# One-bank PSUM tiles in attention and the first MLP, two- and three-bank tiles only in the second, and a longer transfer time in the instruction planner

## The chip, the cores and the metric

One core of a Trainium2 chip runs the kernel as one launch. The metric is the device time in microseconds (us) of that core. A core has five engines with instruction streams of their own: TensorE (PE in the profile, with its weight loads as PEld), VectorE (DVE), ScalarE (ACT), GpSimd (POOL) and SyncE (SP), which here issues the DMA transfers. They wait for each other by semaphores. TensorE writes its products into PSUM, which has eight banks of 128 partitions by 512 fp32 values.

## The reference

All data are fp32. Three stages follow one another: an attention with a block-causal mask, an MLP with a leaky ReLU, and an MLP with SiLU.

```python
# q, k, v: 4 x 8 heads x 576 x 64
scores = (1.0 / np.sqrt(64)) * np.matmul(q, k.transpose(0, 1, 3, 2))
mask = (pos[:, None] // 64) >= (pos[None, :] // 64)
scores = np.where(mask, scores, -1000000000.0)
attn = np.exp(scores - np.max(scores, axis=-1, keepdims=True))
attn = attn / (np.sum(attn, axis=-1, keepdims=True) + 1e-09)
x = np.matmul(attn, v)            # heads joined: 2304 tokens x 512

h = x @ w_in                      # 512 -> 2048
y = np.maximum(0.01 * h, h) @ w_out   # 2048 -> 512

h = y @ w_in2                     # 512 -> 2048
out = (h * (1.0 / (1.0 + np.exp(-h)))) @ w_out2   # 2048 -> 512
```

## The kernel before, in words

**Precision.** Most fp32 products are made from two parts of each factor (a rounded high part and the rest), as three matmuls summed in PSUM; the rounding is done by copies on ACT, DVE and POOL (line L343) and the rests by subtractions (L359). The weights of the second MLP come in as 64-bit words, of which DVE, ACT and POOL make the two parts (the conversions: wraw is the raw load, cy and cc are steps of them; L387 to L416).

**Attention and first MLP.** The 2304 tokens are cut into six blocks of 384. For each block the attention units make scores (L942, L937; in the first block L1123) in a PSUM bank, DVE finds the row maximum (L951; first block L1131, L1142) and masks, ACT takes the exponential out of that bank (L959; first block L1136), and the result meets v (L1000 to L1002). The first MLP then goes through 16 chunks of 128 of its hidden width, with its output in four banks (L1242). Attention of one block is interleaved with the MLP of another.

**Second MLP.** It is multiplied by the Strassen-Winograd scheme: of a pair of chunks and a pair of blocks, seven products instead of eight, in the order 1, 2, 6, 7, 5, 4, 3. The first layer (`add_first`) has 3 x 8 = 24 such pairs, each of 7 products of 6 matmuls of 384 columns (L1471 to L1473); the last (`add_last`, L1634) has five groups of eight pairs, the results summed in PSUM over a group. Product 1 lies in the bank x, products 2 and 6 in s, and products 7, 4, 5 and 3 in acc. After each pair (after each group in the last layer) ACT copies product 1 and DVE combines the products in four steps, each two banks at a time but for the last: `op1` (L1496; products 2 and 6), `op2` (L1499; products 7 and 5), `op3` (L1503; products 4 and 5) and `op4` (L1507; product 3). In the last layer these are L1654, L1660, L1664 and L1669. ACT then applies the SiLU (L1523), and the result goes out to DRAM and comes back for the last layer, as do the converted weights (w2k, L594) and the operands y.

**PSUM.** acc is one tile of four banks for the whole kernel, s one tile of two banks; x and h have one bank each. In attention the scores use the two banks of s by turns, and the first block's transposes use the four of acc by turns.

**What sets the order.** Each engine's stream is ordered by a planner at build time (`class Schedule`): each piece of work has a rank, a cost in ns and the pieces it depends on, and of the pieces that are ready the one with the lowest rank goes next. A transfer counts as its size over 360 bytes per ns and 1500 ns on top (`HOP`). The planner only orders. The semaphores that the chip waits on are made afterwards, from which tiles each instruction reads and writes.

Of the kernel before, what the change touches and what calls it, by code (L numbers as in the profile page):

```python
# [19 lines left out]
P = 128  # L20
# [26 lines left out]
ORDER = (1, 2, 6, 7, 5, 4, 3)  # L47
BEHIND = 6
KQR, KR, QR, VR = 960, 1728, 2048, 1792
# [7 lines left out]
class Task:  # L57
    def __init__(self, engines, deps, rank, emit):
        self.engines, self.deps, self.rank, self.emit = engines, deps, rank, emit
        self.users, self.next, self.waits, self.ready, self.end = [], [], 0, 0.0, None  # L60


class Schedule:
# [23 lines left out]
    def run(self):  # L87
# [20 lines left out]
        while left:  # L108
# [107 lines left out]
def attn_mlp_mlp(  # L216
# [43 lines left out]
    turn_s = [1]  # L260

    def acc_bank(i):
        return acc_all[:, i * 512 : (i + 1) * 512]

# [31 lines left out]
    def next_s():  # L296
        turn_s[0] ^= 1
        return s_all[:, turn_s[0] * 512 : (turn_s[0] + 1) * 512]

# [75 lines left out]

    def convert(src, f, sl, rk, load_rank, to=None, slow=0):

# [39 lines left out]

        t_load = dma(raw_free, load_rank, DM * P * 8, load, after=raw_after, slow=slow)
        raws.takers.append(t_load.issue)
# [169 lines left out]
    def last_raw(f, rk):  # L589

        d, t_x, users = convert(w2, f, slice(DM, 2 * DM), rk, rk - CONV_LOAD / 4)

        def store():
            nc.sync.dma_start(out=w2_kept[f], in_=d["x"])  # L594

        w2_there[f] = dma([t_x], SHORT + rk, P * DM * 4, store)
        users.append(w2_there[f])
# [3 lines left out]
    def last_pair(p, rk, free):  # L601
# [3 lines left out]
        for i in (0, 1):  # L605
# [4 lines left out]
            busy = load_users[p % 2] if p > 1 else y_there[NBLK - 1]  # L610
            t_in.append(dma([w2_there[2 * p + i], *busy], rk - LAST_AHEAD, P * DM * 4, load))
            users.append([])
# [424 lines left out]
    def start():  # L1037
# [318 lines left out]
    def bank(m, n):  # L1356
        if m == 1:
            return x_all[:, :n]
        if m in (2, 6):
            at = (m == 6) * 512  # L1360
            return s_all[:, at : at + n]
        at = (7, 4, 5, 3).index(m) * 512
        return acc_all[:, at : at + n]

    def banks_of(m, n):

        if m == 2:
            return s_all.rearrange("p (k q) -> p k q", q=512)[:, :, :n]
        both = acc_all.rearrange("p (k q) -> p k q", q=512)
        return both[:, 0:3:2, :n] if m == 7 else both[:, 1:3, :n]  # L1370

# [19 lines left out]
    def x_operands(b):  # L1391
# [11 lines left out]
        for k in range(4):  # L1403
# [6 lines left out]
            follow = [t_in[-1].issue] if t_in else []  # L1410
            t_in.append(dma([*y_there[blk][c : c + 2], *free], rk - X2_AHEAD, P * TWO * 4, load, after=follow))

# [44 lines left out]
    def add_first(b, i):  # L1457
# [52 lines left out]
        t1 = plan.add({"DVE": dve_psum(2 * n)}, [t0, t[6], *e_free], r, op1)  # L1510
        t2 = plan.add({"DVE": dve_psum(2 * n)}, [t1, t[5]], r, op2)
        t3 = plan.add({"DVE": dve_psum(2 * n)}, [t2, t[4]], r, op3)
        t4 = plan.add({"DVE": dve_psum(n)}, [t2, t[3]], r, op4)
        bank_free.update({1: [t0], 2: [t1], 6: [t1], 7: [t2], 5: [t3], 4: [t3], 3: [t4]})
        there = []
        first = lambda: d["e0"][:, :n]
        for out_, m, deps, to in (
# [10 lines left out]
            tg = plan.add({"ACT": act(m)}, deps, r, gated)  # L1528
            there.append(dma([tg], SHORT + rk, P * m * 4, store))
        e3_free[k] = [t2, *there]  # L1530
# [12 lines left out]
    def operands4(g, i):  # L1543
# [10 lines left out]
        for side in (0, 1):  # L1554
# [10 lines left out]
            follow = [t_in[0].issue] if t_in else after  # L1565
            t_in.append(dma([*g2_there[i, b], *free], GATE + rk - 3, P * 2 * n * 4, load, after=follow))
        raws.takers.append(t_in[-1].issue)
# [49 lines left out]
    def add_last(g, i):  # L1617
# [54 lines left out]
        t1 = plan.add({"DVE": dve_psum(2 * w)}, [t0, t[6]], r, op1)  # L1672
        t2 = plan.add({"DVE": dve_psum(2 * w)}, [t1, t[5], *c_free["b"]], r, op2)
        t3 = plan.add({"DVE": dve_psum(2 * w)}, [t2, t[4], *c_free["c"]], r, op3)
        t4 = plan.add({"DVE": dve_psum(w)}, [t2, t[3]], r, op4)
        bank_free.update({1: [t0], 2: [t1], 6: [t1], 7: [t2], 5: [t3], 4: [t3], 3: [t4]})
        r0 = 2 * g * TOK
        stored = {}
        for which, at, side, col, dep in (("a", 0, 0, 0, t1), ("c", 0, 1, 0, t3), ("c", 1, 1, 1, t3), ("b", 2, 0, 1, t4)):
# [4 lines left out]

            stored.setdefault(which, []).append(dma([dep], SHORT + rk, P * w * 4, store))
        c_free["a"], c_free["b"], c_free["c"] = [t2, *stored["a"]], [t3, t4, *stored["b"]], stored["c"]
# [126 lines left out]
```

## Time and profile before

| | |
|---|---|
| median of three runs | 1037.62 us (1036.26 to 1041.85) |
| profiled execution | 1036.65 us, its span 1034.9 us, so 1.75 us around it |
| busy in the span | PE 93%, DVE 76%, ACT 54%, POOL 26% |
| attention of the first block | 0 to about 60 us |
| attention and first MLP | about 60 to 620 us |
| second MLP, first layer | about 620 to 839 us |
| second MLP, last layer | about 839 us to the end |

A stage's table of windows says how long each engine was busy in it and at which clock TensorE ran (PEclk, 1.00 is the higher of its two levels). The list of waits sums, for each pair of a waiting line and a line that ended the wait, the idle time. The timeline gives single instructions with, in brackets, the idle time of their engine before them and what ended it. Matmuls overlap, so the distance of two starts, not the duration of one, is what a matmul takes of PE's time.

### The profile page before, as it was taken

The numbers are of one execution on the slowest core, as the hardware profiler recorded it, in microseconds if no ns is written. First come the engines' busy times: TensorE is split into PE (matmuls) and PEld (weight loads), VectorE is DVE, ScalarE is ACT, GpSimd is POOL, SyncE is SP. The second block draws the span as 40 slices with busy tenths as digits, with TensorE's granted clock in tenths as the row PEclk, the third lists the DMA queues.
The fourth block names the chain that finished last, engine by engine and source line by source line (L and its number), as shares of the span: only waits on it lengthen the run. The fifth ranks groups of instructions, "written<-read, shape, count | busy, mean of one in ns | idle before, by whom it ended". The sixth has DMA issues, their size and how long they took to land. (4 is left out here: it accounts for less than half of the span.)

```text
span 1034.9 us, 18465 instructions
## 1 busy us (share of the span) xinstructions
PE 962.2 (93%) x6507; PEld 872.1 (84%) x6507; DVE 785.1 (76%) x1702; ACT 555.0 (54%) x1235; POOL 264.9 (26%) x325
## 2 busy tenths in 40 slices
PE   6788999999999999999999997898889899999997
PEld 3555556899898999899999997888888889999997
DVE  4798898877788878777746696776756788888864
ACT  4678667766777666666645454554345452121222
POOL 1254347212111114011210354323334540000000
PEclk9899999999999999999999998998999999999999
DMA  7576963555665565558424234577635544343422
GB/s 241 170 208 172 212 152 77 129 127 113 141 127 115 135 143 120 117 126 193 114 45 141 72 108 146 184 268 263 207 125 172 176 140 126 125 133 106 139 62 82
DMA packets 193917, 148.81 MB, mean 144 GB/s; under 512 B 134432, under 2 KB 171808, under 8 KB 193824
## 3 DMA queue, kind: packets, MB, share of 16 engines
q1 hardware_dynamic: 193824, 147.63, 52.5%
q8 instruction: 51, 0.84, 0.3%
q14 instruction: 42, 0.34, 0.1%
HBM read 90.44 MB, written 32.51 MB: 119 GB/s over the span
## 5 line engine op out<-in xcount | busy, mean ns | idle before, releaser
L959 ACT ACTIVATE p<-s,st 128x288 f32<-128x288 f32 (+5 forms) x144 | 73.5, 512 | 52.6 <-DVE st L951 33.5
L978 DVE SCALAR_TENSOR_TENSOR hl<-p,st,hl 128x576 f16<-128x576 f32 (+6 forms) x120 | 80.5, 674 | 15.2 <-ACT hl L973 13.4
L1242 PE MATMUL acc<-ghi,w 128*128 128x384 f32 x340 | 88.8, 337 | 0.0
L973 ACT ACTIVATE hl<-p,st 128x576 f16<-128x576 f32 (+6 forms) x118 | 70.0, 598 | 28.5 <-DVE st L969 10.9
L1523 ACT ACTIVATE e<-e 128x384 f32<-128x384 f32 (+1 forms) x72 | 42.9, 627 | 72.1 <-DVE e L1503 52.1
L1270 ACT ACTIVATE g<-h 128x384 f32<-128x384 f32 x96 | 46.6, 486 | 60.0 <-PE h L1224 56.5
L1000 PE MATMUL x<-pt,v 128*128 128x128 f16 (+1 forms) x432 | 69.3, 211 | 6.6 <-DMA pt<-hl 3.5
L359 DVE TENSOR_TENSOR glo<-g,ghi 128x384 fp32r<-128x384 f32 x80 | 53.3, 667 | 26.6 <-ACT ghi L343 25.7
L1001 PE MATMUL x<-pt,v 128*128 128x128 f16 (+1 forms) x432 | 67.1, 209 | 0.0
L1002 PE MATMUL x<-pt,v 128*128 128x128 f16 (+1 forms) x432 | 65.8, 209 | 0.0
L942 PE MATMUL s<-k,q 128*128 128x288 f32 (+7 forms) x256 | 58.7, 331 | 6.2 <-ACT p L959 5.2
L1222 PE MATMUL h<-h,w 128*128 128x384 f32 x180 | 61.1, 339 | 0.0
L1242 PEld LDWEIGHTS acc<-ghi,w 128*128 128x128 f32 x340 | 60.8, 188 | 0.3
L1000 PEld LDWEIGHTS <-v 128*128 128x128 bf16 x432 | 41.3, 98 | 17.9 <-issue 13.0
L1471 PE MATMUL acc<-l,w 128*128 128x384 f32 x90 | 33.5, 372 | 23.0 <-DVE g L1499 22.0
L1242 PE MATMUL acc<-glo,w 128*128 128x384 f32 x160 | 53.7, 336 | 0.3 <-DVE glo L359 0.3
L1224 PE MATMUL h<-h,w 128*128 128x384 f32 x160 | 53.6, 335 | 0.0
L1223 PE MATMUL h<-l,w 128*128 128x384 f32 x160 | 53.6, 335 | 0.0
L359 POOL TENSOR_TENSOR v<-v 128x320 f32<-128x320 f32 (+5 forms) x56 | 39.6, 714 | 51.4 <-DMA v<-vL 44.1
L394 ACT ACTIVATE cy<-wraw 128x512 f32<-128x512 f32 x64 | 42.5, 667 | 18.0 <-DMA wraw<-w 9.2
L1001 PEld LDWEIGHTS <-v 128*128 128x128 bf16 x432 | 41.6, 99 | 9.7 <-issue 9.0
L951 DVE TENSOR_REDUCE st<-s 128x1 f32<-128x320 f32 (+5 forms) x96 | 46.6, 485 | 3.1
(342 smaller groups left out, 3153.7 us busy)
## 6 DMA issues: line engine op xcount, KB each, us to landing
wraw<-w SPq DMA_DIRECT2D x64, 512.0 KB, 4.4
a<-g SPq DMA_DIRECT2D x64, 256.0 KB, 3.2
g<-e SPq DMA_DIRECT2D x48, 192.0 KB, 2.7
g<-e SPq DMA_DIRECT2D x24, 384.0 KB, 2.4
kqr<-kq_l SPq DMA_DIRECT2D x16, 480.0 KB, 3.7
v<-vL SPq DMA_DIRECT2D x32, 160.0 KB, 3.7
y<-yT SPq DMA_DIRECT2D x12, 384.0 KB, 3.6
w2k<-cc SPq DMA_DIRECT2D x16, 256.0 KB, 4.1
```

Of the source, the lines that this page charges most:

```text
L359: engine[e].tensor_tensor(lo, x, hi, op=ALU.subtract)
L942: nc.tensor.matmul(s[:, :w], hd.q[:, a : a + P], hd.k[:, k0:k1], start=i + j == 0, stop=i == len(parts) - 1 and j == 1,)
L959: nc.scalar.activation(p[:rows, k0:k1], u.s[i][:rows, :w], AF.Exp, bias=nm[:rows], accum_out=s2[:rows, i : i + 1])
L973: nc.scalar.activation(hl[:rows, 0, :n], p[:rows], AF.Copy, scale=rc[:rows])
L978: nc.vector.scalar_tensor_tensor(hl[:rows, 1, :n], p[:rows], rc[:rows], hl[:rows, 0, :n], op0=ALU.mult, op1=ALU.subtract)
L1000: nc.tensor.matmul(g.x[:, o], a, hi, start=j == 0, stop=False)
L1001: nc.tensor.matmul(g.x[:, o], hd.vb[:, j], hi, start=False, stop=False)
L1002: nc.tensor.matmul(g.x[:, o], a, lo, start=False, stop=j == nj - 1)
L1222: nc.tensor.matmul(h, w1_lo[s.f][:, sl], hi[:, c, : s.n], start=c == 0, stop=False)
L1223: nc.tensor.matmul(h, w1_hi[s.f][:, sl], lo[:, c, : s.n], start=False, stop=False)
L1224: nc.tensor.matmul(h, w1_hi[s.f][:, sl], hi[:, c, : s.n], start=False, stop=c == NC - 1)
L1242: nc.tensor.matmul(s.acc[c][:, : s.n], a, b, start=s.f == 0 and i == 0, stop=s.f == NF - 1 and i == 2)
```

## The change

No arithmetic is added or taken away. The four-bank acc and the two-bank s no longer exist from the start. In attention each score unit takes a tile of one bank from a pool of two (`ps_s`), and the first block's transposes take one-bank tiles from a pool of four (`ps_t`). When the first MLP starts, the latter gives way to a tile of three banks, acc (products 7, 4 and 5 in the second MLP), and one of a single bank, u (product 3, and the fourth bank of the first MLP's output). When the second MLP starts, the score pool gives way to a two-bank tile s for products 2 and 6. The planner is told that op2 also depends on product 4, and that the bank of product 7 comes free with op3 instead of op2. And it adds 2500 ns (`LAG`) after each transfer of the second MLP: loads of weights and operands, stores and reloads of w2k and of the gated results, and stores of the output.

```diff
-BEHIND = 6
+BEHIND, LAG = 6, 2500
...
-                    u.ready = max(u.ready, t.end + (self.HOP[e] if u in t.users else 0))
+                    u.ready = max(u.ready, t.end + (self.HOP[e] + t.lag if u in t.users else 0))
...
-    acc_all = ps_acc.tile([P, 4 * 512], F32, tag="acc", name="acc")
-    s_all = ps_s.tile([P, 2 * 512], F32, tag="s", name="s")
+    early_s, early_acc = ExitStack(), ExitStack()
+    ps_s = early_s.enter_context(tc.tile_pool(name="ps_s", bufs=2, space=PSUM, side="right"))
+    ps_t = early_acc.enter_context(tc.tile_pool(name="ps_t", bufs=4, space=PSUM))
...
+    banks = {}
+
+    def bank_tile(name, n, side):
+
+        if name not in banks:
+            (early_acc if side == "left" else early_s).close()
+            pool = ctx.enter_context(tc.tile_pool(name=f"ps_{name}", bufs=1, space=PSUM, side=side))
+            banks[name] = pool.tile([P, n * 512], F32, tag=name, name=name)
+        return banks[name]
 
     def acc_bank(i):
-        return acc_all[:, i * 512 : (i + 1) * 512]
+        if i == 3:
+            return bank_tile("u", 1, "left")
+        return bank_tile("acc", 3, "left")[:, i * 512 : (i + 1) * 512]
...
     def next_s():
-        turn_s[0] ^= 1
-        return s_all[:, turn_s[0] * 512 : (turn_s[0] + 1) * 512]
+        return ps_s.tile([P, 512], F32, tag="s", name="s")
...
-    def dma(deps, rank, size, emit, issue=600, after=(), slow=0):
+    def dma(deps, rank, size, emit, issue=600, after=(), slow=0, lag=0):
         t = plan.add({"SP": issue}, deps, rank, lambda e: emit(), after)
         done = plan.add({"DMA": size / 360}, [t], rank, lambda e: None)
+        done.lag = lag
...
-                    u.t = acc_bank(i % 4)
+                    u.t = ps_t.tile([P, 512], F32, tag="t", name="pt0")
...
-            return s_all[:, at : at + n]
-        at = (7, 4, 5, 3).index(m) * 512
-        return acc_all[:, at : at + n]
+            return bank_tile("s", 2, "right")[:, at : at + n]
+        return acc_bank((7, 4, 5, 3).index(m))[:, :n]
...
-        t2 = plan.add({"DVE": dve_psum(2 * n)}, [t1, t[5]], r, op2)
+        t2 = plan.add({"DVE": dve_psum(2 * n)}, [t1, t[5], t[4]], r, op2)
...
-        bank_free.update({1: [t0], 2: [t1], 6: [t1], 7: [t2], 5: [t3], 4: [t3], 3: [t4]})
+        bank_free.update({1: [t0], 2: [t1], 6: [t1], 7: [t3], 5: [t3], 4: [t3], 3: [t4]})
```

The last two edits stand in `add_first` and, alike, in `add_last`; `lag=LAG` stands in the calls of `dma` and `convert` that are named above. Apart from names the streams of all engines are the same up to the first conversions for the second MLP, some 500 us into the run. The lines of the kernel after are 9 or 10 higher than those of the kernel before.

At the start of the second MLP, ACT copies the output of the first MLP's last block out of acc (l is the target) before products 7, 4, 5 and 3 can use these banks; e is a gated result of product 2's and 6's sums, w and cy are weights. Before, ACT's stream reads:

```order
L343 ACTIVATE s1_6913<-x_94 128x384
L343 ACTIVATE w21_1559<-cc_249 128x512
L394 ACTIVATE cy_6940<-wraw_6900 128x512
L1523 ACT_TABLE_LOAD
L1523 ACTIVATE e_6937<-e_6937 128x384
L343 ACTIVATE l_6945<-acc_92 128x384 x4
L394 ACTIVATE cy_6961<-wraw_6909 128x512
```

And now:

```order
L353 ACTIVATE s1_7089<-x_92 128x384
L353 ACTIVATE w22_1637<-t_7066 128x512
L353 ACTIVATE l_7122<-acc_659 128x384
L1532 ACT_TABLE_LOAD
L1532 ACTIVATE e_7119<-e_7119 128x384
L353 ACTIVATE l_7122<-acc_659 128x384 x2
L353 ACTIVATE l_7122<-u_663 128x384
L404 ACTIVATE cy_7157<-wraw_7098 128x512
```

One of the four copies has moved ahead of the load of the activation table and the first SiLU, the three others stay behind both, the last of them from the tile u; the conversion of raw weights that stood before the table load now follows.

On DVE, in the stage of the 24 pairs some 90 us after its start, the conversions of raw weights (cc, cy, wraw) stand between the four combining steps of the pairs (e from s; g from acc; e from acc; e2). Before:

```order
L1507 TENSOR_TENSOR e2_7593<-acc_92,g_175 128x384
L404 TENSOR_SCALAR cc_249<-wraw_7562 128x512
L1496 TENSOR_TENSOR e_6937<-s_93,s1_7591 128x768
L407 TENSOR_SCALAR cc_249<-wraw_7562 128x512
L411 TENSOR_SCALAR cy_7605<-cy_7605 128x512
L404 TENSOR_SCALAR cc_249<-wraw_7571 128x512
L1499 TENSOR_TENSOR g_175<-acc_92,e_6937 128x768
L407 TENSOR_SCALAR cc_249<-wraw_7571 128x512
L1503 TENSOR_TENSOR e_6937<-acc_92,g_175 128x768
L1507 TENSOR_TENSOR e2_7655<-acc_92,g_175 128x384
```

And now, at about the same time of the stage by the pairs:

```order
L369 TENSOR_TENSOR t2_6771<-y_6597,t1_6731 128x768
L421 TENSOR_SCALAR cy_7782<-cy_7782 128x512
L414 TENSOR_SCALAR cc_253<-wraw_7673 128x512
L417 TENSOR_SCALAR cc_253<-wraw_7673 128x512
L1505 TENSOR_TENSOR e_7119<-s_7082,s1_7771 128x768
L1508 TENSOR_TENSOR g_173<-acc_659,e_7119 128x768
L417 TENSOR_SCALAR cc_253<-wraw_7706 128x512
L1512 TENSOR_TENSOR e_7119<-acc_659,g_173 128x768
L1516 TENSOR_TENSOR e2_7850<-u_663,g_173 128x384
```

Before, a step of a conversion (L404) that writes into the area cc stands straight ahead of op2 (L1499), and L407 between op2 and op3. Now nothing stands between op1 (L1505) and op2 (L1508), and one step of a conversion between op2 and op3 (L1512).

On SP's queue at the same place the raw loads (L387), the loads of the operands y for the second pair of blocks (L1407), the stores of converted weights (w2k, L594) and of gated results (g2, L1526) follow each other. Before:

```order
L1526 DMA g2_6_0_129<-e_6937 128x768
L1526 DMA g2_6_0_129<-e2_7440 128x384
L594 DMA w2k6_141<-cc_249 128x512
L1407 DMA y_6418<-yT4_63 128x768
L1526 DMA g2_7_0_132<-e_6937 128x384
L1407 DMA y_6418<-yT5_64 128x768
L1407 DMA y_6418<-yT4_63 128x768
L1526 DMA g2_7_0_132<-e_6937 128x768
L1526 DMA g2_7_0_132<-e2_7531 128x384
L1526 DMA g2_0_1_112<-e_6937 128x384
L387 DMA wraw_7562<-w2 128x512
L387 DMA wraw_7571<-w2 128x512
```

And now:

```order
L1535 DMA g2_7_0_130<-e_7119 128x384
L397 DMA wraw_7673<-w2 128x512
L1416 DMA y_6597<-yT5_64 128x768
L1416 DMA y_6597<-yT4_63 128x768
L397 DMA wraw_7706<-w2 128x512
L1416 DMA y_6597<-yT5_64 128x768
L1535 DMA g2_7_0_130<-e_7119 128x768
L1535 DMA g2_7_0_130<-e2_7709 128x384
L604 DMA w2k5_138<-cc_253 128x512
L604 DMA w2k6_139<-cc_253 128x512
L1535 DMA g2_0_1_110<-e_7119 128x384
L397 DMA wraw_7761<-w2 128x512
```

The loads of raw weights and of y have moved ahead of the stores of the last pair of the first third (g2_7_0), and the stores w2k come later: w2k5 and w2k6 now stand behind the loads of y, where w2k6 stood before them.

## Rows read from the trace of the kernel before

**Rows 1.** Stages: window, length, busy time by engine, PEclk, DMA share, GB/s.

```profile
0.00:60.00 60.00, 43.95 (x213) 28.00 (x214) 37.12 (x114) 35.48 (x98) 13.60 (x23) 0.91 0.63 209
60.00:170.00 110.00, 104.03 (x565) 62.77 (x564) 95.35 (x251) 81.96 (x198) 54.99 (x65) 0.98 0.69 166
620.20:839.20 219.00, 191.68 (x1035) 183.73 (x1034) 155.81 (x223) 104.17 (x180) 85.79 (x65) 0.96 0.56 188
```

**Rows 2.** PE's waits, whole span: waiter, releaser, total us, times, longest.

```profile
PE acc L1471 <- DVE g L1499: 22.0, 18, 3.5
PE s L1123 <- ACT e L1136: 6.2, 5, 3.2
PE s L942 <- ACT p L959: 5.2, 8, 1.3
PE acc L1471 <- ACT l L343: 3.5, 2, 2.6
...
PE s L937 <- ACT p L959: 3.4, 3, 1.9
PE acc L1634 <- DVE l L1669: 3.1, 4, 0.8
PE s L1123 <- DVE small L1142: 2.8, 2, 1.6
...
PE acc L1634 <- DVE e L1664: 2.1, 4, 0.6
PE acc L1634 <- DVE l L1660: 2.1, 2, 1.3
...
PE acc L1471 <- DVE e L1507: 1.4, 3, 0.7
```

**Rows 3.** Timeline of one pair: start, us, engine, line, [idle before <-releaser].

```profile
752.57 0.96 DVE L1499 TENSOR_TENSOR g<-acc,e 128x768 f32<-128x768 f32 x1 [1.43 <-PE acc L1473]
...
753.59 0.44 PE L1471 MATMUL acc<-l,w 128*128 128x384 f32 x1 [1.05 <-DVE g L1499]
...
754.75 0.34 PE L1471 MATMUL x<-x,w 128*128 128x384 f32 x1
...
754.95 0.96 DVE L1503 TENSOR_TENSOR e<-acc,g 128x768 f32<-128x768 f32 x1 [1.42 <-PE acc L1473]
...
757.88 0.33 PE L1471 MATMUL acc<-h,w 128*128 128x384 f32 x1
...
762.21 0.44 PE L1471 MATMUL acc<-l,w 128*128 128x384 f32 x1 [1.05 <-DVE g L1499]
```

**Rows 4.** Timeline of PE at the start of MLP2's products.

```profile
628.29 0.44 PE L1471 MATMUL acc<-h,w 128*128 128x384 f32 x1 [2.58 <-ACT l L343]
```

**Rows 5.** Timeline of DVE and PE at the longest wait of the stage.

```profile
714.58 0.46 DVE L404 TENSOR_SCALAR cc<-wraw 128x512 uint16<-128x512 uint32 x1 [3.52 <-DMA w2k<-cc]
...
715.93 0.69 PE L1471 MATMUL acc<-l,w 128*128 128x384 f32 x1 [3.47 <-DVE g L1499]
```

**Rows 6.** Windows of the slow clock: columns as in the first group.

```profile
630.00:638.00 8.00, 6.31 (x19) 5.80 (x20) 2.26 (x4) 2.37 (x5) 0.05 (x1) 0.50 0.37 117
716.00:720.00 4.00, 4.00 (x13) 4.00 (x14) 1.98 (x4) 0.70 (x1) 0.00 (x0) 0.50 0.64 197
```

**Rows 7.** Shapes on DVE, 640 to 835: count, busy, mean ns, idle before.

```profile
L359 DVE TENSOR_TENSOR xw<-t,xw 128x768 fp32r<-128x768 f32 x2 | 3.5, 1744 | 0.0
...
L359 DVE TENSOR_TENSOR y<-y 128x768 f32<-128x768 f32 x1 | 0.9, 948 | 0.0
```

**Rows 8.** Timeline of DVE and PE at a group's end in the last layer.

```profile
879.42 1.23 DVE L1660 TENSOR_TENSOR l<-acc,l 128x1024 f32<-128x1024 f32 x1 [0.73 <-PE acc L1634]
...
880.89 1.22 DVE L1664 SCALAR_TENSOR_TENSOR e<-acc,l 128x1024 f32<-128x1024 f32 x1
...
882.16 0.50 PE L1634 MATMUL acc<-w,h 128*128 128x256 f32 x2 [0.63 <-DVE e L1664]
```

**Rows 9.** DMA issues: queue, count, KB each, us to landing.

```profile
w2k<-cc SPq DMA_DIRECT2D x16, 256.0 KB, 4.1
```

More of the change, by code (lines that the diff above doesn't have):

```diff
@@ L60, in __init__ @@
         self.users, self.next, self.waits, self.ready, self.end = [], [], 0, 0.0, None
+        self.lag = 0
 class Schedule:
@@ L374, in attn_mlp_mlp, with convert @@
     raws, cys, ccs = Turns(RAWS), Turns(CYS), Turns(CCS)
-    def convert(src, f, sl, rk, load_rank, to=None, slow=0):
+    def convert(src, f, sl, rk, load_rank, to=None, slow=0, lag=0):
         d = {}
@@ L416, in added @@
             engine[e].tensor_tensor(d["x"].bitcast(I32), d["y"].bitcast(I32), ci, op=ALU.add)
-        t_load = dma(raw_free, load_rank, DM * P * 8, load, after=raw_after, slow=slow)
+        t_load = dma(raw_free, load_rank, DM * P * 8, load, after=raw_after, slow=slow, lag=lag)
         raws.takers.append(t_load.issue)
@@ L589, in last_raw @@
     def last_raw(f, rk):
-        d, t_x, users = convert(w2, f, slice(DM, 2 * DM), rk, rk - CONV_LOAD / 4)
+        d, t_x, users = convert(w2, f, slice(DM, 2 * DM), rk, rk - CONV_LOAD / 4, lag=LAG)
         def store():
             nc.sync.dma_start(out=w2_kept[f], in_=d["x"])
-        w2_there[f] = dma([t_x], SHORT + rk, P * DM * 4, store)
+        w2_there[f] = dma([t_x], SHORT + rk, P * DM * 4, store, lag=LAG)
         users.append(w2_there[f])
@@ L610, in last_pair @@
             busy = load_users[p % 2] if p > 1 else y_there[NBLK - 1]
-            t_in.append(dma([w2_there[2 * p + i], *busy], rk - LAST_AHEAD, P * DM * 4, load))
+            t_in.append(dma([w2_there[2 * p + i], *busy], rk - LAST_AHEAD, P * DM * 4, load, lag=LAG))
             users.append([])
@@ L1360, in bank @@
             at = (m == 6) * 512
-            return s_all[:, at : at + n]
-        at = (7, 4, 5, 3).index(m) * 512
-        return acc_all[:, at : at + n]
+            return bank_tile("s", 2, "right")[:, at : at + n]
+        return acc_bank((7, 4, 5, 3).index(m))[:, :n]
     def banks_of(m, n):
         if m == 2:
-            return s_all.rearrange("p (k q) -> p k q", q=512)[:, :, :n]
-        both = acc_all.rearrange("p (k q) -> p k q", q=512)
-        return both[:, 0:3:2, :n] if m == 7 else both[:, 1:3, :n]
+            return banks["s"].rearrange("p (k q) -> p k q", q=512)[:, :, :n]
+        three = banks["acc"].rearrange("p (k q) -> p k q", q=512)
+        return three[:, 0:3:2, :n] if m == 7 else three[:, 1:3, :n]
     def twice(a):
@@ L1410, in x_operands @@
             follow = [t_in[-1].issue] if t_in else []
-            t_in.append(dma([*y_there[blk][c : c + 2], *free], rk - X2_AHEAD, P * TWO * 4, load, after=follow))
+            t_in.append(dma([*y_there[blk][c : c + 2], *free], rk - X2_AHEAD, P * TWO * 4, load, after=follow, lag=LAG))
         def t1(e):
@@ L1528, in add_first @@
             tg = plan.add({"ACT": act(m)}, deps, r, gated)
-            there.append(dma([tg], SHORT + rk, P * m * 4, store))
+            there.append(dma([tg], SHORT + rk, P * m * 4, store, lag=LAG))
         e3_free[k] = [t2, *there]
@@ L1565, in operands4 @@
             follow = [t_in[0].issue] if t_in else after
-            t_in.append(dma([*g2_there[i, b], *free], GATE + rk - 3, P * 2 * n * 4, load, after=follow))
+            t_in.append(dma([*g2_there[i, b], *free], GATE + rk - 3, P * 2 * n * 4, load, after=follow, lag=LAG))
         raws.takers.append(t_in[-1].issue)
@@ L1672, in add_last @@
         t1 = plan.add({"DVE": dve_psum(2 * w)}, [t0, t[6]], r, op1)
-        t2 = plan.add({"DVE": dve_psum(2 * w)}, [t1, t[5], *c_free["b"]], r, op2)
+        t2 = plan.add({"DVE": dve_psum(2 * w)}, [t1, t[5], t[4], *c_free["b"]], r, op2)
         t3 = plan.add({"DVE": dve_psum(2 * w)}, [t2, t[4], *c_free["c"]], r, op3)
         t4 = plan.add({"DVE": dve_psum(w)}, [t2, t[3]], r, op4)
-        bank_free.update({1: [t0], 2: [t1], 6: [t1], 7: [t2], 5: [t3], 4: [t3], 3: [t4]})
+        bank_free.update({1: [t0], 2: [t1], 6: [t1], 7: [t3], 5: [t3], 4: [t3], 3: [t4]})
         r0 = 2 * g * TOK
@@ L1683, in store @@
                 nc.sync.dma_start(out=o.rearrange("(s p) d -> p s d", p=P), in_=v)
-            stored.setdefault(which, []).append(dma([dep], SHORT + rk, P * w * 4, store))
+            stored.setdefault(which, []).append(dma([dep], SHORT + rk, P * w * 4, store, lag=LAG))
         c_free["a"], c_free["b"], c_free["c"] = [t2, *stored["a"]], [t3, t4, *stored["b"]], stored["c"]
```

7 lines of the change are left out of this document (2 added, 5 removed).

## The prediction, made before the changed kernel was run

> **What bounds the kernel now.** I read the table of stages first, then the list of TensorE's waits, then timelines where waits are long. TensorE (PE) bounds every stage: in the first layer of the second MLP it is busy 191.68 of 219.00 us, DVE 155.81, ACT 104.17, POOL 85.79 [rows 1]. So the time is PE's matmuls plus what PE loses between them, and the reader should see how unequally that loss is spread. The list of waits [rows 2] has one large row: 22.0 us in 18 waits of L1471 for L1499, longest 3.5. All others are below 7. The first layer's floor shows how much there is to win: between 754.75 and 757.88 us 18 matmuls start, 0.1739 us each [rows 3], so the 1035 matmuls of the stage cost 180.0 us at the full clock; 39.0 of its 219.0 are lost.
>
> The timeline of one pair tells what that large wait is [rows 3]. The matmul at 753.59 is the first of product 3. It has waited for L1499, which is op2, and op2 reads the banks of products 7 and 5, not that of product 3. Op2 itself, at 752.57, had waited 1.43 us for PE, until product 4 was done, which it doesn't read either; op3, at 754.95, waited for product 3. So the dependences hold for the whole four-bank tile, not for its banks, and PE and DVE take turns on it. From one such wait to the next 8.62 us pass (753.59 to 762.21), for 42 matmuls that need 7.30: 1.32 per pair, of which 1.05 show as idle and 0.27 as a slow first matmul behind it (0.44 instead of 0.34) and its weight load.
>
> **The change part by part.**
>
> *First layer, the tile u.* Product 3 now has a tile of its own, and waits only for op4 of the pair before, which is over six products earlier. The 18 waits go: 22.0 us shown, and 18 x 0.27 = 4.9 behind them, together 26.9. Bounds: 22.0 (the restart cost stays) to 26.9; I take 26.9, since a matmul without a wait starts at 0.1739.
>
> *What is late next.* Op2 still shares a tile with product 4, op3 with nothing new, and the next pair's product 7 now waits for op3, in the same tile of three banks. Behind product 4 PE still has 3, then 1, 2 and 6 of the next pair: 24 matmuls, 4.17 us. In that time DVE must do op2 and op3, 0.96 each [rows 3], with at most one other instruction between by the order shown: some 2.4 us with the hops, so 1.8 us of slack. Where DVE is late, PE waits. The nearest row is product 7 waiting for L1507, the last of the four steps: 1.4 us in three waits, in 24 pairs [rows 2]. Bounds: none, to the longest of those (about 0.65) in each of 24 pairs, 15.6 us. I take 5, a third of it: more than the row, since DVE's 155.81 us will fill 82% of a stage of some 190 us instead of 71%. The 1.4 us for L1507 shrink by 1.0, as op4 no longer holds product 7.
>
> *Start of the layer.* PE waits 3.5 us for ACT's copies of the first MLP's output [rows 2], 2.58 of it at 628.29 [rows 4]. One copy now precedes the table load, but three still follow it. Bounds 0 to 2.2; I take 1.1.
>
> *The clock.* In this stage the granted clock was 0.50 in 630 to 638 and 716 to 720 [rows 6], 12 us at the lower level, so 6.0 us lost. The first stretch comes after the 2.58 us of idle at 628.29, the second after 3.47 us at 715.93 [rows 4, 5]. The waits of 1.05 us left the pair of rows 3 at 0.1739 per matmul. With the second wait gone and the first shorter I take all 6.0 back; bounds 2 (716 to 720 alone) to 6.
>
> First layer: 26.9 + 1.1 + 1.0 + 6.0 - 5 = 30 us.
>
> *Last layer.* Here the pattern comes once per group. PE's waits for L1669, L1664 and L1660 are 3.1 + 2.1 + 2.1 = 7.3 us in ten waits [rows 2]; with 0.27 behind each, 10.0. At 882.16 product 7 waited for op3 (L1664, 1.22 us), which followed an op2 that had itself waited for the tile until 879.42 [rows 8]. Now op2 can start with the end of product 4, about one product of 0.72 us earlier; op3 then ends when PE needs the bank. I take 8, bounds 5 (product 7 still waits at each end) to 10.
>
> *Attention.* Scores in one of the two s banks waited for the exponential out of the other, again one tile. In the first block the waits are 6.2 + 2.8 = 9.0 us (L1123), in the later ones 5.2 + 3.4 = 8.6 (L942, L937) [rows 2]. With a tile per bank they reach back two units instead of one. But the exponential needs the row maximum on DVE first, and DVE is busy 95.35 of 110 us from 60 to 170 [rows 1]: what PE gains it may wait for elsewhere. Bounds 0 to 9.0 and 0 to 8.6; I take 5 and 6, somewhat over half.
>
> *The added 2500 ns.* They change no transfer, only when the planner believes data to be there; loads go out earlier and their users come later. That is what the three pairs of streams show. Before, DVE stood 3.52 us at a conversion (L404) that had to write over an area whose store w2k was still under way, and op2 stood behind it in the queue, with PE behind op2 [rows 5]. The conversion stood straight ahead of op2; now none stands there. That wait is in the 22.0 already, so I count nothing more. Bounds: nothing, to minus 3.5 if one such stall comes back.
>
> The stores w2k of 256 KB landed after 4.1 us in the median [rows 9], and the one in the way took longer. The Trainium skill (DMA: Bandwidth & Descriptors, "Anatomy of one DMA — SWDGE (gpsimd) path") gives a transfer about 2.0 us fixed and its bytes at 436 GB/s, an estimate of 2.6 us for 256 KB; by that a lag of 2500 ns more would only push work back, and the sum would lose the 3.5 us counted in the wait. These transfers are issued by SP, not by GpSimd, and the measured 4.1 is longer, so the 3.5 stay in the sum.
>
> **Sum.** 30 + 8 + 5 + 6 = 49 us from the profiled 1036.65 (its span 1034.9 and 1.75 around it) is 987.65. The median of the runs lies 0.97 higher, so I say 988.5.
>
> **Rivals.**
>
> *R1, DVE takes the place.* If product 7 waits for op3 in most pairs, the 15.6 us replace my 5, and part of the restart cost and of the clock stays lost (some 4): the first layer gives 15, the time is about 1003.5. For it: DVE's combining steps share its queue with operand work of very unequal length, L359 at 128x768 0.948 us once and 1.744 in the mean of another two [rows 7]. Against it: 1.8 us of slack. The Trainium skill (SBUF — State Buffer, "Who interferes with whom") says that a DVE instruction with two SBUF inputs contends with GpSimd's reads and one with a single SBUF input doesn't; the two L359 lengths fit that, and op2, with one input in PSUM, kept 0.96.
>
> *R2, attention gives nothing.* The freed scores wait for row maxima or for transposed exponentials instead, as nothing else on their path becomes shorter. The 5 and the 6 of the sum fall out: 999.5. For it: DVE's 95.35 of 110 us; against it: PE was idle just there.
>
> *R3, all of it comes.* No new wait (5 more), all of attention's waits (6.6 more), the last layer whole (2 more), and 5 for the restarts behind attention's waits and the clock in the first block: about 970.
>
> *R4, slower.* The planner's later users leave operands of the pairs too late: raw weights come in three buffers, and a conversion planned behind a longer transfer can put the high and low parts of w behind PE's need. The nearest price is the stall at 628.29, 2.58 us with the clock falling behind it. It decides from 19 pairs of 24 on (49 / 2.58); in all 24, with the clock's loss of 4 at two or three of them, it would come to some 1046. Against it: the list of waits has no row in which L1471 waits for a weight or an x; its three rows are those of [rows 2]. The kernel not doing what it says is near to R2: it would need the dependences to stay by bank pairs, and the streams show u as its own tile.
>
> **How the numbers follow.** My forecast, 975 to 1000 on its own, has 0.60; R1 0.15; R2 0.12; R3 0.07; R4 0.03; no change, by gains that are all given back later, 0.03. The range takes in R1, and R2 wholly, and leaves half of R3 and all of R4 out: 974 to 1008. Faster by over 0.5% (5 us, about what runs of this kernel can tell from no change) holds with forecast, R1, R2 and R3, 0.94; within it 0.03; slower 0.03.
>
> **What would show it.** Right: no wait of product 3 for op2; op2 and op3 next to each other behind product 4; pairs of 7.3 us; the stage of the 24 pairs near 190 us, with PEclk at 1.00 but for its start; waits of scores (L952, L947 now) below 7 us in all. Wrong: a row of product 7 waiting for op3 above 10 us (R1); scores waiting as long as before, for DVE (R2); TensorE waiting for w or x from ACT, DVE or POOL in the 24 pairs (R4).

## The result, and the profile after

The changed kernel took 977.7 us (median of four runs, 977.12 to 980.62) beside 1036.94 us of the kernel before (four runs): a ratio of 0.9425, interval 0.939 to 0.9461. The forecast was 988.5, with a range of 974 to 1008. The profiled execution took 980.62 us with a span of 978.9, 56.0 us less than before. One execution of e7 below took 3687.46 us and is left out of its row.

Four landmarks on TensorE split these 56.0 us: the first matmul of the first MLP (L1217, now L1227), the first product of the second MLP (L1471, now L1480), the first matmul of product 2 in the last layer (into s; L1634, now L1643) and the end.

| stretch, us | before | after | gain | forecast |
|---|---|---|---|---|
| start to the first MLP | 58.2 | 44.8 | 13.4 | 5 |
| from there to the second MLP | 562.2 | 559.2 | 3.0 | 6 |
| first layer, 24 pairs | 217.7 | 185.2 | 32.5 | 30 |
| last layer to the end | 196.9 | 189.7 | 7.2 | 8 |

The windows of the kernel after, the last one around its longest wait in the first layer (columns as in [rows 1]):

```profile
0.00:44.80 44.80, 37.68 (x207) 24.02 (x208) 36.05 (x112) 33.47 (x94) 12.80 (x23) 1.00 0.79 268
604.00:790.80 186.80, 181.66 (x1036) 179.94 (x1035) 159.85 (x225) 101.05 (x178) 88.86 (x67) 0.99 0.65 222
790.80:978.90 188.10, 181.36 (x1500) 180.03 (x1498) 151.00 (x229) 53.16 (x70) 2.84 (x3) 0.99 0.39 119
672.00:676.00 4.00, 2.97 (x10) 3.00 (x11) 4.00 (x6) 2.36 (x4) 2.98 (x2) 0.65 0.97 337
```

The window of the first layer is 32 us shorter than that of [rows 1], while DVE's busy time in it has hardly changed: 159.85 us where [rows 1] have 155.81. So DVE is now busy for 86% of it instead of 71%. The list of TensorE's waits, to be laid beside [rows 2]:

```profile
PE x L1010 <- DMA pt<-hl: 6.6, 8, 1.8
PE x L1010 <- DVE x L841: 4.0, 2, 3.0
PE acc L1480 <- DVE e L1512: 2.9, 2, 2.7
PE s L1133 <- ACT e L1146: 2.9, 3, 1.5
PE acc L1480 <- ACT l L353: 1.8, 2, 1.3
...
PE acc L1643 <- DVE l L369: 1.0, 1, 1.0
...
PE acc L1643 <- DVE e L1673: 0.8, 1, 0.8
PE s L952 <- ACT p L969: 0.7, 1, 0.7
...
PE s L947 <- ACT p L969: 0.5, 1, 0.5
```

The wait for op2 (22.0 us before) has no row any more. The two rows of scores that wait for the exponential (L952, L947) have shrunk from 8.6 to 1.2 us, and in the last layer 0.8 us are left (L1673) of the 7.3 for the combining steps, with 1.0 us for an operand step (L369). A part has come back elsewhere: attention's products with v (L1010) wait 6.6 us for the transposing transfer and 4.0 for DVE, where the kernel before had 3.5 and 2.6 (L1000).

The timeline of one pair, DVE and TensorE, answers to [rows 3]:

```profile
699.83 0.96 DVE L1508 TENSOR_TENSOR g<-acc,e 128x768 f32<-128x768 f32 x1 [1.22 <-PE acc L1482]
...
700.67 0.33 PE L1480 MATMUL x<-x,w 128*128 128x384 f32 x1
...
700.82 0.96 DVE L1512 TENSOR_TENSOR e<-acc,g 128x768 f32<-128x768 f32 x1
...
703.79 0.33 PE L1480 MATMUL acc<-h,w 128*128 128x384 f32 x1
...
706.91 0.33 PE L1480 MATMUL u<-l,w 128*128 128x384 f32 x1
...
707.44 0.95 DVE L1508 TENSOR_TENSOR g<-acc,e 128x768 f32<-128x768 f32 x1
...
707.95 0.33 PE L1480 MATMUL x<-x,w 128*128 128x384 f32 x1
...
708.64 0.95 DVE L1512 TENSOR_TENSOR e<-acc,g 128x768 f32<-128x768 f32 x1
...
711.07 0.33 PE L1480 MATMUL acc<-h,w 128*128 128x384 f32 x1
```

The pair's first product starts at 700.67 and the next pair's at 707.95, so 7.28 us pass, what 42 matmuls need. Product 3 (u, at 706.91) starts without a bracket. Op2 (699.83) and op3 (700.82) follow each other behind product 4; op3 is over 2.0 us before product 7 starts at 703.79, and in the pair after it (op3 at 708.64, product 7 at 711.07) 1.5 us before. In 19 of the 23 distances between pairs the trace has these 7.28 us.

The one long wait that is left in the first layer is of the kind that rival R1 named. Timeline of DVE, POOL and TensorE there:

```profile
666.92 2.60 DVE L369 TENSOR_TENSOR h<-y,h 128x768 fp32r<-128x768 f32 x1
...
668.67 2.54 POOL L369 TENSOR_TENSOR l<-y,l 128x768 fp32r<-128x768 f32 x1
...
669.44 0.94 DVE L1508 TENSOR_TENSOR g<-acc,e 128x768 f32<-128x768 f32 x1
...
670.31 1.71 DVE L369 TENSOR_TENSOR h<-t,h 128x768 fp32r<-128x768 f32 x1
...
671.94 0.94 DVE L1512 TENSOR_TENSOR e<-acc,g 128x768 f32<-128x768 f32 x1
...
673.03 0.49 PE L1480 MATMUL acc<-h,w 128*128 128x384 f32 x1 [2.71 <-DVE e L1512]
```

Op2 stands in DVE's queue behind operand steps of the next x. One of these (L369, 128x768) takes 2.60 us beside POOL's own of the same line, another 1.71 between op2 and op3, where [rows 7] show 0.948 for this shape, at a moment when POOL did nothing. Product 7 waits 2.71 us for op3, and the granted clock of the window 672 to 676 is 0.65. A wait of this length happens once, in this profile and in the second one of the same kernel (e9).

### The profile page after: what moved, and what is told of

It reads as the page before. It is cut to its first block, busy times and chain, and to the rows that moved or that the text cites. A ratio compares the mean times of both kernels' runs of the same rounds, so it can differ in the third digit from the quotient of the medians.

```text
span 978.9 us, 18468 instructions
## 1 busy us (share of the span) xinstructions
PE 946.3 (97%) x6507; PEld 866.8 (89%) x6507; DVE 786.2 (80%) x1700; ACT 554.3 (57%) x1235; POOL 265.5 (27%) x327
## 4 chain that ended last, share of the span: by engine, by line
PE 52%; DVE 2%; DMA 2%; issue 1%; ACT 1%; DVEq 0%; SPq 0%; ACTq 0%
PE acc L1643 7%; PE acc L1252 6%; PE s L1643 5%; PE h L1232 3%; PE h L1233 3%; PE h L1234 3%; PE acc L1480 3%; PE acc L1481 2%; PE acc L1482 2%; PE x L1643 2%; PE u L1643 2%; PE u L1252 2%; PE s L1480 2%; PE s L1482 2%; PE s L1481 2%; DMA pt<-hl 1%
## 5 line engine op out<-in xcount | busy, mean ns | idle before, releaser
L969 ACT ACTIVATE p<-s,st 128x288 f32<-128x288 f32 (+5 forms) x144 | 73.4, 512 | 45.4 <-DVE st L961 31.1
L1010 PE MATMUL x<-pt,v 128*128 128x128 f16 (+1 forms) x432 | 69.4, 212 | 11.7 <-DMA pt<-hl 6.6
L369 DVE TENSOR_TENSOR glo<-g,ghi 128x384 fp32r<-128x384 f32 x80 | 53.5, 669 | 29.3 <-ACT ghi L353 28.4
L1252 PE MATMUL acc<-ghi,w 128*128 128x384 f32 x255 | 66.7, 337 | 0.0
L1010 PEld LDWEIGHTS <-v 128*128 128x128 bf16 x432 | 41.2, 98 | 23.2 <-issue 14.6
L952 PE MATMUL s<-k,q 128*128 128x288 f32 (+7 forms) x256 | 58.3, 329 | 0.8 <-ACT p L969 0.7
L369 POOL TENSOR_TENSOR v<-v 128x320 f32<-128x320 f32 (+5 forms) x55 | 38.3, 702 | 48.6 <-DMA v<-vL 48.2
L1011 PEld LDWEIGHTS <-v 128*128 128x128 bf16 x432 | 41.6, 99 | 10.4 <-issue 9.0
L404 ACT ACTIVATE cy<-wraw 128x512 f32<-128x512 f32 x64 | 42.6, 668 | 9.4 <-DMA wraw<-w 2.4
L1252 PEld LDWEIGHTS acc<-ghi,w 128*128 128x128 f32 x255 | 45.5, 188 | 0.3
L816 POOL MEMSET v<- 128x320 bf16 (+2 forms) x56 | 21.0, 384 | 88.1 <-DVE v L369 61.8
L993 POOL MEMSET hl<- 128x128 f16 x64 | 12.5, 205 | 111.7 <-DMA pt<-hl 89.1
```

The lines of the kernel that those rows point to most:

```text
L369: engine[e].tensor_tensor(lo, x, hi, op=ALU.subtract)
L969: nc.scalar.activation(p[:rows, k0:k1], u.s[i][:rows, :w], AF.Exp, bias=nm[:rows], accum_out=s2[:rows, i : i + 1])
L1010: nc.tensor.matmul(g.x[:, o], a, hi, start=j == 0, stop=False)
L1011: nc.tensor.matmul(g.x[:, o], hd.vb[:, j], hi, start=False, stop=False)
L1252: nc.tensor.matmul(s.acc[c][:, : s.n], a, b, start=s.f == 0 and i == 0, stop=s.f == NF - 1 and i == 2)
```

## The experiments

Twelve kernels ran. In the first eight one part of the change is undone, or done alone. The last four columns give the stretches above, of the profiled execution alone. Each ratio is to runs of the kernel before that were made beside it.

| kernel | median us (range) | ratio to before, interval | start | to second MLP | first layer | last layer |
|---|---|---|---|---|---|---|
| before | 1036.94 (1035.97 to 1041.85) | 1 | 58.2 | 562.2 | 217.7 | 196.9 |
| after | 977.7 (977.12 to 980.62) | 0.9425, 0.939 to 0.9461 | 44.8 | 559.2 | 185.2 | 189.7 |
| e1 scores joined | 1003.99 (998.18 to 1007.72) | 0.9653, 0.9609 to 0.9697 | 57.5 | 562.6 | 186.5 | 189.9 |
| e2 acc and u joined | 991.44 (990.26 to 994.5) | 0.9542, 0.9507 to 0.9577 | 44.7 | 557.4 | 189.9 | 198.1 |
| e3 transposes joined | 976.4 (971.77 to 978.15) | 0.9386, 0.9352 to 0.942 | 47.1 | 553.0 | 185.2 | 189.7 |
| e4 lag 0 | 981.5 (979.95 to 982.39) | 0.944, 0.9414 to 0.9466 | 45.4 | 553.0 | 190.8 | 189.0 |
| e5 no planner deps | 975.19 (972.67 to 978.53) | 0.9396, 0.9361 to 0.9431 | 44.6 | 555.1 | 180.8 | 192.3 |
| e6 u alone | 1006.5 (1001.48 to 1007.91) | 0.9684, 0.965 to 0.9718 | 59.5 | 567.8 | 188.8 | 189.9 |
| e7 planner deps alone | 1023.2 (1020.46 to 1023.31, three runs) | 0.9845, 0.9816 to 0.9875 | 58.4 | 566.5 | 199.2 | 197.4 |
| e8 lag alone | 1035.28 (1031.57 to 1041.57) | 0.9968, 0.994 to 0.9996 | 59.8 | 562.3 | 211.9 | 199.8 |
| e9 after again | 976.85 (973.33 to 979.2) | 0.9394, 0.937 to 0.9418 | 44.4 | 554.1 | 184.9 | 189.7 |
| e10 no planner deps again | 975.07 (974.79 to 977.27) | 0.9384, 0.936 to 0.9408 | 44.6 | 556.4 | 182.3 | 192.3 |
| e11 tiles alone | 980.91 (976.34 to 984.35) | 0.9431, 0.9403 to 0.9459 | 44.5 | 554.2 | 189.6 | 189.8 |
| e12 lag 4000, no deps | 989.09 (985.01 to 991.15) | 0.951, 0.9485 to 0.9536 | 45.3 | 554.1 | 192.7 | 195.5 |

**e1: the score banks joined again** (the edit, on the kernel after):

```diff
-        return ps_s.tile([P, 512], F32, tag="s", name="s")
+        turn_s[0] ^= 1
+        return s_both[:, turn_s[0] * 512 : (turn_s[0] + 1) * 512]
```

> The kernel after, with only the score tiles undone: the attention scores use the two banks of one tile by turns again; acc, u and the transposes stay as after, and so does the order of instructions. Theory (the start's 13.4 us and attention's 2.9 us came from the scores no longer waiting for the unit just before): about 12 of these 16 us come back, 988 to 993 us, with PE's waits of the first block's scores for ACT and DVE at 9 us or more and the first matmul of the first MLP at 55 to 58 us instead of 44.8. Rival (the start gained because the transposes of the first block have a tile for each bank): below 981 us, first matmul of the first MLP below 48 us.

The start is 57.5 us long again. TensorE's waits in this kernel (L1136 are the first block's scores, L955 and L950 the later ones):

```profile
PE s L1136 <- ACT e L1149: 6.2, 4, 3.2
PE s L955 <- ACT p L972: 6.0, 12, 1.2
...
PE s L950 <- ACT p L972: 3.5, 5, 1.3
...
PE s L1136 <- DVE small L1155: 2.8, 2, 1.6
```

They are those of [rows 2] within 1 us. The start's gain belongs to the score tiles. The time rose by more than either expectation: in the profiled execution, 998.18, the later attention too is back at 562.6 us, where e9, the kernel after once more, has 554.1. The other three took 4 to 9 us more, and their mean granted clock was lower: 0.990 at 998.18, 0.985 at 1002.42, 0.983 at 1005.56 and 0.980 at 1007.72. One hundredth of some 1000 us is 10 us, so the clock can account for this spread; in which stretch it fell no profile shows.

**e3: the transposes joined** (one tile of four banks by turns instead of `ps_t`):

```diff
-                    u.t = ps_t.tile([P, 512], F32, tag="t", name="pt0")
+                    u.t = t_all[:, i % 4 * 512 : (i % 4 + 1) * 512]
```

> The kernel after, with only the transposes' tiles undone: the first block's transposes use the four banks of one tile by turns, as before the change; the rest stays, and the order too. Theory (the scores' tiles make the start shorter): 977 to 981 us, first matmul of the first MLP at 45 to 48 us. Rival (the transposes' tiles make it): 986 to 991 us, that matmul at 53 to 58 us.

Nothing is lost: 976.4 us. The start is 2.3 us longer in its profile and the stretch behind it shorter by more, within the spread of that stretch.

**e2: acc and u joined**

```diff
-        if i == 3:
-            return bank_tile("u", 1, "left")
-        return bank_tile("acc", 3, "left")[:, i * 512 : (i + 1) * 512]
+        return bank_tile("acc", 4, "left")[:, i * 512 : (i + 1) * 512]
```

> The kernel after, with only u undone: acc is one tile of four banks again from the first MLP on; score tiles, transposes, lag and the order of instructions stay. Theory (product 3 waited for op2 because the tile is one): the waits of product 3 for op2 come back, some 18 x 1.05 and their restarts in the first layer and 6 to 8 us in the last, and the clock falls where one is long: 1005 to 1014 us, a pair 8.4 to 8.7 us long. Rival (the first layer gained because the new order puts op2 and op3 next to each other and the conversions elsewhere): below 988 us, with waits of product 3 below 8 us in all.

Both theories missed. The last layer lost its gain whole (198.1), as the theory has it, but the first layer lost only 4.7 of its 32.5 us, and no wait of product 3 for op2 came back. TensorE's waits in the two layers (L1514 is op4, L1676 op4 of the last layer):

```profile
PE acc L1478 <- DVE e L1514: 7.0, 4, 4.2
PE acc L1641 <- DVE l L1676: 5.8, 4, 2.1
...
PE acc L1641 <- DVE e L1514: 2.7, 1, 2.7
```

Product 7 waits for op4 instead. The traces show what has turned round. In the kernel before, op2 starts ahead of product 3 in 18 of the 24 pairs, and these are the 18 waits of [rows 2]; in the other six it starts 0.04 us behind the end of product 3, which has not waited. In e2 it starts behind product 3 in all 24, as in this pair, with product 3's last matmul and op2 (L1506):

```profile
651.98 0.33 PE L1480 MATMUL acc<-l,w 128*128 128x384 f32 x1
...
652.35 0.96 DVE L1506 TENSOR_TENSOR g<-acc,e 128x768 f32<-128x768 f32 x1 [1.11 <-PE acc L1480]
```

The reason that fits is that dependences follow the order in which the planner writes work down, over all engines; this order itself stands in no trace. Before, op2 depended on product 5 but not on product 4, so it could be written between products 4 and 3, and product 3, which writes into the tile that op2 reads, had to wait for it. With the planner's new dependence on product 4, op2 is written behind product 3. Then op2 waits for product 3, even in a tile of four banks, and not the other way round. That made a new theory, A: either the tile u or the planner's edit alone takes the wait away. Four kernels tested it.

**e4 and e8: the lag taken out of the kernel after, and put alone into the kernel before** (`LAG = 0`; `LAG = 2500` with nothing else)

> The kernel after, with LAG 0: tiles and the planner's two new dependences stay, the order is that of a planner without the 2500 ns. Theory (the lag only moves single stalls of DVE behind a transfer): 978 to 984 us, one or two waits of 2 to 4 us of DVE or PE behind a transfer in the first layer of the second MLP. Rival (the lag carries a good part of the gain in that layer): above 988 us, with waits for transfers spread over its pairs.

> The kernel before, with the lag of 2500 ns and nothing else. Theory A: product 3 still waits for op2 in about 17 pairs, 1.05 us each; the one stall of 3.5 us and the slow clock behind it go: a first layer of 210 to 217 us, 1030 to 1038 us. Rival C: a first layer of 190 to 200 us, 1010 to 1020 us.

Without the lag the first layer is 5.6 us longer (190.8), with it alone 5.8 shorter (211.9). There the waits of product 3 stay, one fewer and none of 3.5 us:

```profile
PE acc L1477 <- DVE g L1505: 20.5, 17, 2.8
```

So the lag is worth some 5 us of the first layer by itself, and does not carry the change. DVE's waits in the first layer show what it takes away; before, e8, e4, after:

```profile
DVE cc L404 <- DMA w2k<-cc: 3.5, 1, 3.5
...
DVE cc L411 <- DMA w2k<-cc: 0.3, 1, 0.3
...
DVE cc L414 <- DMA w2k<-cc: 6.7, 4, 2.9
...
DVE cc L414 <- DMA w2k<-cc: 0.4, 1, 0.4
```

Without the lag, conversions on DVE stand behind stores of w2k that are under way; with it next to nothing of this is left. On TensorE the difference shows in two places. Its waits in this layer fell from 26.9 to 24.7 us in e8, and from 7.8 (e4) to 4.7 us in the kernel after. The clock was at its lower level for 17.0 us before and 6.8 us in e8, for 6.8 in e4 and 3.4 after, and half of that time is lost. This makes 2.2 + 5.1 us for e8 and 3.1 + 1.7 for e4, where the layer changed by 5.8 and 5.6: a sum that is about right in the second and 1.5 us too large in the first.

**e5: the planner's two dependences undone in the kernel after**

```diff
-        t2 = plan.add({"DVE": dve_psum(2 * n)}, [t1, t[5], t[4]], r, op2)
+        t2 = plan.add({"DVE": dve_psum(2 * n)}, [t1, t[5]], r, op2)
...
-        bank_free.update({1: [t0], 2: [t1], 6: [t1], 7: [t3], 5: [t3], 4: [t3], 3: [t4]})
+        bank_free.update({1: [t0], 2: [t1], 6: [t1], 7: [t2], 5: [t3], 4: [t3], 3: [t4]})
```

> The kernel after, with the planner's two new dependences undone (op2 on product 4, bank 7 free with op3); tiles and lag stay. Theory A (the tile u alone takes away product 3's wait for op2; so does the planner's dependence alone, because it lets op2 be written down behind product 3, and then op2 waits for product 3 and not the other way round): 976 to 983 us, no wait of product 3 for op2. Rival B (the planner's dependence carries the first layer's gain, u only the last layer's): 998 to 1008 us.

975.19 us, just under the range expected, with a first layer of 180.8: with u, the dependences are not needed.

**e6: u alone** (the kernel before, with acc of three banks and a tile u)

```diff
-        return acc_all[:, i * 512 : (i + 1) * 512]
+        return u_all if i == 3 else acc_all[:, i * 512 : (i + 1) * 512]
```

> The kernel before, with product 3 (and the fourth bank of the first MLP's output) in a tile u of its own, and nothing else: score tiles, planner and lag of before. Theory A: the first layer takes 186 to 192 us instead of 218, the last 190 instead of 197: 998 to 1005 us beside 1037 to 1040 of before. Rival B: a first layer of 208 us or more, 1022 us or more.

The first layer took 188.8 us, the last 189.9: u alone gives 28.9 and 7.0 us, as theory A has it; the time, 1006.5, is 1.5 us above its range. Product 7 waits little for op3 (L1503):

```profile
PE acc L1471 <- DVE e L1503: 3.4, 3, 1.6
```

**e7: the planner's dependences alone** (the two lines of e5 the other way, in the kernel before)

> The kernel before, with the planner's two new dependences and nothing else: all tiles of before, lag 0. Theory A: product 3 is written down ahead of op2 and no longer waits for it though the tile is one; op2 waits for product 3 instead, and product 7 for op4: a first layer of 188 to 196 us, a last of 197, 1008 to 1016 us. Rival C (only a tile of its own takes the wait away; what was left of the gain without u came from the lag): a first layer above 208 us, 1028 us or more.

The wait of product 3 is gone here too, with all tiles as before, and op2 starts behind product 3 in all 24 pairs: theory A's mechanism, and against rival C. But the time, 1023.2, lies between their ranges, since only 18.5 of the first layer's us come of it (a layer of 199.2 us, 188 to 196 expected), and nothing in the last layer. TensorE's waits for op4 (L1507, L1669), and one of them in the timeline:

```profile
PE acc L1471 <- DVE e L1507: 10.7, 10, 2.8
PE acc L1634 <- DVE l L1669: 6.0, 4, 2.3
...
PE acc L1634 <- DVE e L1507: 2.5, 1, 2.5
```

```profile
699.77 0.94 DVE L1503 TENSOR_TENSOR e<-acc,g 128x768 f32<-128x768 f32 x1
700.64 0.54 DVE L1507 TENSOR_TENSOR e<-acc,g 128x384 f32<-128x384 f32 x1
...
701.32 0.41 PE L1471 MATMUL acc<-h,w 128*128 128x384 f32 x1 [2.67 <-DVE e L1507]
```

Op2 now starts behind product 3, one product later, and product 7 waits for op4, one step later than with u. In pairs where nothing stands between the steps, product 7 starts 0.5 us behind op4, where the kernel after has 2.0 us behind op3. One step of 1.25 us between them uses that up, and in place of the 22.0 us a wait of 10.7 us stands.

**e9 to e12: the version without the planner's dependences beside the kernel after, and other lags**

> The kernel after, unchanged, beside the next three on one chip: 976 to 981 us, first layer 185 us, with one wait of 2 to 3 us of product 7 for op3 where DVE's operand steps and conversions run beside POOL.

> The kernel after without the planner's two new dependences, once more, now beside the kernel after. Theory (with u the dependences are not needed, and without them no operand step stands between op1 and the late op2 at the change of x): 2 to 5 us faster than the kernel after, first layer 180 to 183 us, no wait of product 7 for op3 above 1 us. Rival (chance between chips and calls): within 1.5 us of it.

> The tiles of the kernel after, with the planner of before (no new dependences, lag 0). Theory (the tiles carry the gain, the lag 3 to 6 us of the first layer): first layer 186 to 191 us, 977 to 984 us. Rival (the lag is worth nothing): within 1.5 us of the same kernel with the lag of 2500 ns.

> As the kernel without the planner's two dependences, with a lag of 4000 ns instead of 2500. If the lag's gain comes from covering the longest transfers (the store in the way took some 7 us): 0 to 3 us faster, first layer 179 to 182 us. Rival (2500 ns covers them, more of it puts users late): 1 to 6 us slower, with waits of TensorE for w or x in the first layer.

On one chip, five rounds, the kernel after has 0.9394 and the one without dependences 0.9384: the intervals lie on each other, and the medians, 1.8 us apart, lie between the theory's 2 to 5 us and the rival's 1.5. Its first layer is 2.7 us shorter, where the wait of 2.71 us is missing, and its last layer 2.6 longer. No version was found that is surely faster than the kernel after. With the tiles alone (lag 0, no dependences) the ratio is 0.9431; the first layer is 4.6 us longer than after, and 7.3 longer than with the lag and no dependences (e10). A lag of 4000 ns costs 14 us against 2500, more than either side had expected: its first layer is 10.4 us longer, with waits for op3 (L1512) and for the high part of an operand that ACT makes (h), as R4 would have it:

```profile
PE acc L1480 <- DVE e L1512: 4.6, 4, 2.3
...
PE acc L1480 <- ACT h L353: 3.2, 1, 3.2
```

## Why the prediction was right, point by point

The range held, but the larger misses all went the same way: the median lies 10.8 us below the point forecast and 7.7 above R3's 970. Attention's waits and the clock of the first block came back in full, as R3 had it, and the lag gave what the forecast had put at nothing.

- **Product 3's wait for op2** (26.9 us forecast): gone, and the pair is at 7.28 us, as forecast. That u takes it away is shown by e6. The forecast's reason, that dependences hold for the tile and not for its banks, was half of it: they also go by the order in which the planner writes, and the planner's edit alone turns this wait round (e7).
- **Product 7's wait for op3** (5 us, bounds 0 to 15.6): 2.9 us in two waits. The slack of 1.8 us by the forecast is 1.5 to 2.0 in the pairs shown; the long wait came where two operand steps of 2.60 and 1.71 us stood before op3. Where u is missing, a neighbour of R1 holds: product 7 waits for op4, the step behind (e7, 10.7 us).
- **The clock** (6.0 us): [rows 6] count 12 us at the lower level, but the trace of before has 17.0, the second stretch from within the wait on:

```profile
629.50:639.70 10.20, 8.12 (x25) 7.50 (x25) 4.23 (x7) 3.21 (x6) 0.55 (x1) 0.50 0.34 109
714.80:721.60 6.80, 5.67 (x18) 5.67 (x19) 3.96 (x8) 2.30 (x5) 0.00 (x0) 0.50 0.66 225
```

  That is 8.5 us lost (PEclk is the third number from the end). After, 3.4 us at the lower level are left, behind the wait of 2.71 us, or 1.7 us lost; so up to 6.8 us came back. In this profile the clock did not fall at the layer's start, where the two waits are now 1.8 us together.
- **First layer** as a whole: 32.5 us, forecast 30. Of these, TensorE's waits make 22.2 (26.9 to 4.7) and the clock 6.8; the 3.5 that remain are about the restarts behind the waits (4.9 forecast). That the sum came out so near is in part luck: tiles alone gave 28.1 (e11), and the lag, counted as nothing, a part of the waits and of the clock.
- **Last layer** (8 us, bounds 5 to 10): 7.2, and by e2 and e6 u's alone.
- **The start** (5 us, bounds 0 to 9.0) is the term that was mis-sized: 13.4, outside its bounds. The bound was made from two of the waits of L1123, 9.0 us, and left out two smaller rows of the same line and the clock. The rows, of the kernel before:

```profile
PE s L1123 <- ACT e L343: 1.3, 1, 1.3
...
PE s L1123 <- DVE small L1131: 1.0, 2, 0.8
```

  TensorE's waits up to the first MLP, its own among them, fell from 16.0 to 7.0 us, 9.0 less. And before, the clock had fallen in two places. Two windows of the kernel before show it, the second behind the wait of 3.2 us:

```profile
12.00:15.00 3.00, 2.94 (x8) 1.64 (x8) 1.08 (x4) 1.28 (x4) 0.00 (x0) 0.50 1.04 413
33.30:39.00 5.70, 5.68 (x18) 4.42 (x19) 2.60 (x8) 2.84 (x6) 1.87 (x6) 0.50 0.29 95
```

  That is 8.7 us of work at half the clock, 4.4 us lost, and after the change PEclk is 1.00 throughout the start. Together 13.4, the whole gain. In the profiles of all five kernels with joined score banks the start has 10 to 14 us at the lower level; in those of the nine with single banks none but for 3.4 us in e3. The doubt that held the term down, that the exponential would wait for DVE instead, did not come true in this stretch.
- **Attention of the later blocks** (6 us): 3.0 between the two profiled executions, but that of the kernel after is not typical: its clock was at the lower level for 10.2 us of this stretch, in e9, the same kernel, for 3.4, and e9's stretch is 5.1 us shorter. Over all kernels with joined score banks this stretch took 562.2 to 567.8 us (five profiles), over those with single banks 553.0 to 559.2 (nine). The means, 564.3 and 555.2, differ by 9.1, about the whole of the 8.6 us of waits. R2 is wrong in all but attention's products with v: for the transfer and DVE they wait 4.7 to 6.1 us in the five, 6.0 to 10.6 in the nine.
- **The lag** (nothing, bounds 0 to minus 3.5): a gain of some 5 us in the first layer (e4, e8), outside the bounds. The stall behind w2k is gone, as said. But the forecast counted it once, as one stall of the kernel before. Without the lag the new tiles have four such waits of DVE, 6.7 us (e4); product 7 waits 4.6 us for op3 where the kernel after has 2.9, and at the layer's start TensorE waits 3.2 us for ACT instead of 1.8. The forecast had put the latter down to the copies of ACT by themselves.
- **R4's price** was added up wrongly: 24 x 2.58 are 61.9 us, on 988.5 some 1050, and about 1060 with the clock's loss, not 1046. A wait of its kind of over 1 us came only with the lag of 4000 ns (e12, 3.2 us).

## What to carry to other kernels

A PSUM tile of several banks is one thing to the tracker of dependences: look in the waits for a writer that waits for a reader of another bank, and give that product a tile of its own. Where the waits are small, a shared tile costs little (the transposes, e3). Where a planner writes the program, the order of writing decides which of the two waits: one more dependence gave 18.5 us of the first layer here, the tile 28.9, and with the tile the dependence was not needed. When a wait is priced, the clock that falls behind it and the small rows of the same line belong to the price.

## What the runs showed of the hardware

A step of DVE with two inputs in SBUF (L369, 128x768) took 0.948 us in one place and 2.60 beside POOL's steps of the same line, while the combining steps with one input in PSUM kept 0.94 to 0.96 within the same microseconds. The forecast had 1.744 as the longer length. The traces of all fourteen kernels bear it out: of DVE's 128x768 steps with both inputs in SBUF, 480 ran while POOL did nothing and took 0.94 to 0.96 us each; 178 had POOL beside them for at least a part, and 116 of these took over 1.2 us, up to 2.61. The 1008 combining steps of that shape stayed at 0.93 to 0.96 us, 596 of them beside POOL.

The clock was at 0.65 on average over 4 us around a wait of TensorE of 2.71 us. At the layer's start the same two waits, 0.58 and 1.28 us, left the clock at its higher level in e9 and were followed by 3.4 us at the lower one in e10, so the waits alone do not tell whether it falls. The matmuls behind the second wait, in e9 and in e10:

```profile
607.04 0.44 PE L1480 MATMUL acc<-l,w 128*128 128x384 f32 x1 [1.28 <-ACT l L353]
...
609.49 0.69 PE L1480 MATMUL acc<-l,w 128*128 128x384 f32 x1 [1.28 <-ACT l L353]
```

A part of the spread between executions of one kernel is the clock's. Of the six of e9 the fastest took 973.33 us at a mean granted clock of 0.997 and the slowest 979.2 at 0.991, and 0.006 of some 975 us is 5.9 us, all of this difference; but another took 978.31 at 0.996, so the clock is not the whole of the spread.
